# First batch of an attention and FFN kernel: block-transposed reciprocals, another order of its units, later weight loads, and more FFN work ahead of the third batch

## The chip, the cores and the metric

The kernel runs on one core of a Trainium2 chip. TensorE (PE in the profile, PEld for its weight loads), VectorE (DVE), ScalarE (ACT) and GpSimd (POOL) compute. SyncE (SP) and POOL issue DMAs. The metric is the time of one execution on the device in microseconds (us). The kernel before took 391.18 us, median of 6 runs (390.0 to 393.7). All other times come from one profiled execution.

## The reference

Attention over 8 batches and 8 heads of 576 queries, with 16 extra keys and values (the beacon) that every query sees; its output, as 4608 tokens by 512, goes through a gated FFN. Cut to what matters:

```python
k_all = concat([beacon_k, k]); v_all = concat([beacon_v, v])       # 592 keys
scores = (q @ k_all.T) / 8, causal on the 576 own keys
a = exp(scores - max); a /= a.sum(-1) + 1e-9
x = (a @ v_all) as [8*576, 8*64]
out = (relu(x @ w_gate) * (x @ w_val)) @ w_out                      # 512 -> 1536 -> 512
```

The result is float32. The kernel computes in bfloat16 with float32 sums.

## The kernel before

**Attention.** A batch has two groups g of four heads. Its 576 queries are cut into three chunks ci of 240, 256 and 80. A unit is one score tile: for a group and a chunk, the scores of one tile kt of 128 keys (small ones share a unit). Each batch has 14 units, two for each of its 7 steps. `Unit.qk` (L330) writes scores to one of two PSUM buffers s. `Unit.exp` (L341) takes exp on ACT (L344) into e, and POOL masks the diagonal (L352). When all units of a (g, ci) are through, `Chunk.av` (L364) multiplies: four heads side by side, 32 columns each, into the bank ab for the values and, with a tile of ones, into the bank os for the sums of exp. So each sum stands 32 times over, in the 32 partitions of its head. `Chunk.invert` (L390) takes the reciprocal of every element of os, and `Chunk.scale` (L395) multiplies ab by it into xT, the FFN's input. `Chunk.note` (L402) folds the reciprocals into a running minimum and maximum, which tell at the end whether a general path must run. ab and os have one buffer each. Chunks of the first batch's second group borrow two f banks or an s tile.

**FFN.** For each 512 tokens 12 up groups (`Ffn.up`, L412: four matmuls with wg at L419, four with wv at L428, relu on ACT, product on VectorE) and 4 down groups (`Ffn.down`, L432: 12 matmuls with wo at L438, a copy, a DMA to out). f banks: two.

**Order.** It is written by hand: `plan` (L474) is a list of steps, each with a batch and its part, or None where only FFN work runs, and a quota of FFN work. A whole-number quota counts groups; another one is in us of TensorE time. `ALONE` (L471) gives the steps without attention: four after the first batch (0, 3, 3 and 2 groups), two after the second (3 and 3). The third batch's steps have a quota of 3.0, later ones 4.4. `BASE` is the first step of each batch; s2, the second's, is step 11. Hooks hang on steps: `between` (behind the first unit's scores), `mid`, `behind`, and `after` (end of the step). Every engine runs its own instructions in this program order.

**Loads.** The first batch's q and k come in quarters (k or q, half i of the rows, group g), loaded by SP as float32 (wide), cast to bfloat16 (hwide), turned by TensorE (L282) and moved to kT and qT (L283). The last 64 rows, the tails, are turned in bank os (L305) and moved (L306). The second batch's quarters come through POOL's casting DMAs (L271), and are turned by TensorE in steps 10 (s2 - 1) and 12. The three weights come through POOL's queue too: `load_w` (L310) brings a third of wg or wv in two DMAs, `load_wo` (L316) half of wo. In POOL's order stand: first wg pair, first wv pair, second pairs, third pairs, the eight hwide loads, then a one-element memset (L227) on the buffer into which SP loads the second batch's first tile of v; SP's later DMAs stand behind that load. From the third batch on `fetch` (L631) loads float32 tiles of 128 rows on SP, POOL casts them (L249), and SP turns them by DMA transpose (L254), interleaved with the DMAs that write out. In these batches the second unit of a group needs key tile 3 and q tiles 2 and 3.

Of the kernel before, what the change touches and what calls it, by code (L numbers as in the profile page):

```python
# [10 lines left out]
FP32 = mybir.dt.float32  # L11
BF16 = mybir.dt.bfloat16
# [4 lines left out]
def general_path(tc, q, k, v, beacon_k, beacon_v, out, ident, wg, wv, wo):  # L17
# [119 lines left out]
)  # L137


UNITS_BY_CHUNK = (  # L140
    ((0, 0, 0),), ((0, 0, 1), (1, 0, 1)), ((1, 0, 0),), ((0, 1, 2),),
    ((0, 1, 3), (1, 1, 3)), ((0, 1, 1),), ((0, 1, 0),), ((1, 1, 2),), ((1, 1, 1),), ((1, 1, 0),),
# [11 lines left out]
def kernel(  # L154
# [12 lines left out]
    nc = tc.nc  # L167
    B, H, S, D = q.shape
    Nb = beacon_k.shape[2]
    P = 128  # L170
# [7 lines left out]
    M_TILE = 512  # L178
    C = 32
# [130 lines left out]
    def load_w(dst, src, n0, n1):  # L310
        for g in range(2):
            nc.gpsimd.dma_start(  # L312
                dst[:, 2 * g:2 * g + 2, n0:n1],
                src[2 * g * P:2 * (g + 1) * P, n0:n1].rearrange("(p a) n -> p a n", a=2))
# [42 lines left out]
    class Chunk:  # L357


        def __init__(self, batch, g, ci):  # L360
            self.batch, self.g, self.ci = batch, g, ci
            self.last = len(CHUNKS[ci][2]) - 1

        def av(self):  # L364
            spare = self.batch.b == 0 and self.g == 1
            if spare and self.ci == 2:
                s = s_ps.tile([P, 2, 2, 256], FP32, name="s")
                self.ab, self.os = s[:, 0], s[:, 1, 0]
            else:
                self.ab = (f_ps if spare else o_ps).tile(  # L370
                    [P, 2, 256], FP32, name="f" if spare else "ab")
                self.os = (f_ps if spare else o_ps).tile(
                    [P, 256], FP32, name="f" if spare else "os")
            cq0, _, segs = CHUNKS[self.ci]
            order = sorted(segs, key=lambda x: x[0])
            for i, (kt, q0, n, _, _) in enumerate(order):
                e = self.batch.e.pop((self.g, self.ci, kt))
                kr = min(P, Stot - kt * P)
                for part in range(3):
                    for hh in range(4):  # L380
                        rows = slice(hh * C, (hh + 1) * C)
                        c0 = (4 * self.g + hh) * D + part * C
                        w = ones[:kr, :] if part == 2 else self.batch.v[:kr, kt, c0:c0 + C]
                        o = self.os[rows] if part == 2 else self.ab[rows, part]
                        nc.tensor.matmul(  # L385
                            o[:, q0 - cq0:q0 - cq0 + n], w, e[:kr, 2 * (hh % 2) + hh // 2],
                            start=(i == 0 and part != 1), stop=(i == self.last),
                            skip_group_check=True)

        def invert(self):  # L390
            n = CHUNKS[self.ci][1]
            self.r = nrm.tile([P, 256], FP32, name="r")
            nc.vector.reciprocal(self.r[:, :n], self.os[:, :n])  # L393

        def scale(self):  # L395
            cq0, n, _ = CHUNKS[self.ci]
# [63 lines left out]
    def count_rows(ok):  # L460
# [7 lines left out]
    later_sp, pools = [], {}  # L468
    STEPS = 7

    ALONE = ((0, 3, 3, 2), (3, 3))  # L471
    BASE = [STEPS * b + sum(map(len, ALONE[:b])) for b in range(B)]

    plan = ([(0, i, 0) for i in range(STEPS)]  # L474
            + [(None, 0, n) for n in ALONE[0]]
            + [(1, i, 1) for i in range(STEPS)]
            + [(None, 0, n) for n in ALONE[1]]
            + [(b, i, 3.0 if b == 2 else 4.4) for b in range(2, B) for i in range(STEPS)]
            + [(None, 0, 4.5)])

    with tc.manual_schedule():
# [16 lines left out]
        def warm_up(count, n):  # L498
            for _ in range(count):
                nc.tensor.matmul(idle_ps[:, :n], wo[:, 0, :P], wo[:, 0, :n],  # L500
                                 start=True, stop=True)
# [12 lines left out]
        warm_up(4, M_TILE)  # L514
        first.turn_rows(first.cast_rows(first.beacon, dve), first.kT[:, :, :Nb], dve)()
        warm_up(2, M_TILE)
        def turn_first(i, g):
            for n in "kq":
                ps = f_ps.tile([P, 2, 2, P], BF16, name="f")
                first.turn_quarter(n, i, g, ps, act if n == "q" and g == 0 else dve)()  # L520
                if i == 0 and n == "k":
                    warm_up(1, 256)

        def cast_first(i, g):
            first.cast_quarter("k", i, g, dve)
            first.cast_quarter("q", i, g, dve if (i, g) == (1, 1) else act)

        cast_first(0, 0)
        turn_first(0, 0)
        warm_up(2, 256)  # L530
        cast_first(0, 1)

        def turn_two(x, i, k_bank):
            ps = {"k": k_bank.tile([P, NP, 2, P], BF16, name="f" if k_bank is f_ps else "s"),
# [9 lines left out]
        def turn_tails(x, move, ps=(None, None)):  # L544
            moves = [x.turn_rows(x.tails[0], x.kT[:, :, 528:592], move, ps[0]),
                     x.turn_rows(x.tails[1], x.qT[:, :, 512:576], move, ps[1])]
            for m in moves:
                m()

        def turn_first_tails():  # L550
            ps = o_ps.tile([P, 2, NP, 64], BF16, name="os")
            turn_tails(first, act, (ps[:, 0], ps[:, 1]))

        later_half, between, behind, mid = {}, {}, {}, {}

        def after(step, action):
            later_half.setdefault(step, []).append(action)
# [3 lines left out]
        load_tails(second)  # L561
        s2 = BASE[1]

        def turn_next():
            turn_first(0, 1)
            warm_up(2, 256)

        between[0] = turn_next
        mid[0] = lambda: cast_first(1, 0)
        after(0, lambda: cast_first(1, 1))  # L570
        after(0, lambda: first.cast("v", 0, pool))
        after(0, lambda: first.cast("v", 1, pool))
        def turn_last():
            turn_first(1, 0)
            ps = o_ps.tile([P, 2, 2, 2, P], BF16, name="ab")
            moves = []
            for x, n in enumerate("kq"):
                moves.append(first.turn_quarter(n, 1, 1, ps[:, x], dve))
                warm_up(1, (M_TILE, 256)[x])
            for move in moves:  # L580
                move()
            cast_tails(first, dve)

        between[1] = turn_last
        after(1, lambda: load_w(wg, moe_w_gate, 0, 512))
        after(2, lambda: first.cast("v", 2, pool))
        after(2, lambda: first.cast("v", 3, pool))
        after(2, lambda: load_w(wv, moe_w_val, 0, 512))
        behind[3] = turn_first_tails
        after(3, lambda: first.cast("v", 4, pool))  # L590
        after(3, lambda: load_w(wg, moe_w_gate, 512, 1024))
        after(4, lambda: load_w(wv, moe_w_val, 512, 1024))
        after(6, lambda: load_w(wg, moe_w_gate, 1024, 1536))
        after(6, lambda: load_w(wv, moe_w_val, 1024, 1536))

# [60 lines left out]
        for s, (b, i, quota) in enumerate(plan):  # L656
# [9 lines left out]
            if b is not None:  # L666
                if i == 0:
                    batches[b].e = {}
                order = UNITS_BY_CHUNK if b < 2 else UNITS_BY_GROUP
                units = [Unit(batches[b], order[2 * i + x]) for x in range(2)]  # L670
            chunks, due = due, []

            def values():
                for c in chunks:
                    c.av()
                    c.invert()
                    if b == 1:
                        c.scale()
                        notes.append(c.note)

            for j, u in enumerate(units):
                u.qk()
                if j == 0 and s in between:
                    between[s]()
                if j == 0 and s in (4, s2 + 1):
                    values()
            if units:
                units[0].exp()
            if units and s in mid:
                mid[s]()  # L690
            if s in behind:
                behind[s]()
            if s not in (4, s2 + 1):
                values()
            if s == STEPS:
                f = f_ps.tile([P, M_TILE], FP32, name="f")
                for _ in range(5):
                    nc.tensor.matmul(f, first.kT[:, 0, :P], first.kT[:, 0, :M_TILE],
                                     start=True, stop=True)
            credit = min(credit + quota, 2 * quota)  # L700
# [13 lines left out]
            for j, (kind, _, run) in enumerate(mine):  # L714
                if j == 0 and other and (kind == "down" or len(mine) == 1):
                    other.pop().exp()
                ups = kinds.count("up")
                run((b is None and j < len(mine) - 1) or (ups > 1 and j == (1 if ups > 2 else 0)))
                if j == 0:
                    for c in chunks if b != 1 else []:  # L720
                        c.scale()
                        notes.append(c.note)
                    if b is None and s in mid:
                        mid[s]()
                if other:
                    other.pop().exp()
                if b is None and notes:
                    notes.pop(0)()
            if not mine:
                for c in chunks if b != 1 else []:  # L730
                    c.scale()
                    notes.append(c.note)
                if other:
                    other.pop().exp()
# [59 lines left out]
```

## Time and profile before

| | |
|---|---|
| median of 6 runs | 391.18 us |
| the profiled execution's own time | 390.64 us |
| its span on the core | 388.9 us |
| busy PE / PEld / DVE / ACT / POOL | 369.4 / 187.7 / 204.8 / 192.0 / 124.2 us |
| PE busy in 16 to 26 us | 6.94 of 10 us |
| PE busy in 82 to 86 us | 1.60 of 4 us |
| moved by DMA | 49.85 MB, mean 128 GB/s |

The first 27 us are the first batch's attention, where no FFN input exists yet. From there FFN groups fill the time between the attention's pieces. TensorE's busy share is near 1 in most stretches, but the clock granted to it can be below full speed, so a busy stretch isn't always full work.

### The profile page before, as it was taken

To read this page: it belongs to the slowest core of one execution; us is meant where nothing else is said; L and a number is where in the kernel's file an instruction comes from. 1 tells how busy PE (TensorE), PEld (TensorE's weight loads), DVE (VectorE), ACT (ScalarE), POOL (GpSimd) and SP (SyncE) were. 2 spreads that over 40 slices of the span, in tenths; PEclk is the share of its full clock that TensorE was granted. 3 is DMA by queue.
4 is the path that set the end of the run, shared out by engine and by line. 5 is a ranking of instruction groups with operands and counts; after the bars stand their busy time and mean duration, and the time that the engine had idled before them with its cause. 6 is when DMAs were issued, how large, how long until landed. Compare 5 with 4: busy or idle time off the path is not lost.

```text
span 388.9 us, 10175 instructions
## 1 busy us (share of the span) xinstructions
PE 369.4 (95%) x4239; PEld 187.7 (48%) x4296; DVE 204.8 (53%) x333; ACT 192.0 (49%) x269; POOL 124.2 (32%) x217
## 2 busy tenths in 40 slices
PE   7779998979999999999999999999999999999995
PEld 3554454434554545445544545454544554444443
DVE  4878476535654566466446553666365654512320
ACT  4763493326655554565546545655465533323321
POOL 1795455325543442254225332335201100000000
PEclk9999999989999999999999999999999999999999
DMA  7999999759977872688267834786200020001002
GB/s 226 194 179 193 208 187 217 172 149 220 175 138 207 181 170 78 174 186 159 71 160 182 166 84 127 185 191 79 98 29 2 2 79 31 2 38 73 0 28 88
DMA packets 146788, 49.85 MB, mean 128 GB/s; under 512 B 133296, under 2 KB 142256, under 8 KB 146736
## 3 DMA queue, kind: packets, MB, share of 16 engines
q1 hardware_dynamic: 137680, 43.37, 47.6%
q0 software_dynamic: 9056, 5.77, 10.6%
q8 instruction: 35, 0.57, 0.7%
q14 instruction: 17, 0.14, 0.1%
HBM read 38.27 MB, written 9.44 MB: 123 GB/s over the span
## 4 chain that ended last, share of the span: by engine, by line
PE 81%; DMA 7%; POOL 4%; SPq 2%; issue 2%; DVE 1%; ACT 1%; POOLq 0%; DVEq 0%
PE f L438 24%; PE f L419 21%; PE f L428 10%; PE s L428 10%; PE s L336 6%; PE ab L385 6%; DMA wo<-in_moe_w_out_dram 3%; PE os L385 2%; DMA raw<-in_v_dram 2%; POOL e L352 1%; POOL v L245 1%; SPq L254 1%; DMA wide<-in_q_dram 1%; SPq L230 1%; POOL wg L312 1%
## 5 line engine op out<-in xcount | busy, mean ns | idle before, releaser
L344 ACT ACTIVATE e<-s 128x1024 bf16<-128x1024 f32 (+2 forms) x112 | 104.3, 966 | 23.3 <-PE s L336 23.3
L419 PE MATMUL f<-xT,wg 128*128 128x512 bf16 x407 | 110.0, 382 | 1.5 <-DVE hT L430 0.3
L422 ACT ACTIVATE g<-f 128x512 f32<-128x512 f32 x108 | 64.6, 598 | 88.2 <-PE f L419 82.6
L438 PE MATMUL f<-wo,hT 128*128 128x512 bf16 (+1 forms) x420 | 94.8, 373 | 3.6 <-issue 1.6
L352 POOL TENSOR_SCALAR_AFFINE_SELECT e<-e 128x512 bf16<-128x512 bf16 (+2 forms) x80 | 46.6, 595 | 153.7 <-ACT e L344 146.2
L393 DVE RECIPROCAL r<-os 128x240 f32<-128x240 f32 (+2 forms) x45 | 61.0, 1355 | 42.0 <-PE os L385 41.9
L430 DVE TENSOR_TENSOR hT<-g,f 128x512 bf16<-128x512 f32 x54 | 37.1, 688 | 60.1 <-PE f L428 54.3
L428 PEld LDWEIGHTS <-wv 128*128 128x128 bf16 x432 | 42.4, 98 | 52.7 <-issue 2.9
L430 DVE TENSOR_TENSOR hT<-g,s 128x512 bf16<-128x512 f32 x54 | 37.1, 688 | 58.3 <-PE s L428 55.2
L438 PEld LDWEIGHTS <-hT 128*128 128x128 bf16 x444 | 41.4, 98 | 47.9 <-issue 1.5
L419 PEld LDWEIGHTS <-wg 128*128 128x128 bf16 x432 | 40.1, 98 | 47.7 <-issue 1.9
L441 ACT COPY ob<-f 128x512 f32<-128x512 f32 (+1 forms) x37 | 21.3, 575 | 73.2 <-PE f L438 73.2
L428 PE MATMUL s<-xT,wv 128*128 128x512 bf16 x213 | 55.6, 382 | 0.1
L428 PE MATMUL f<-xT,wv 128*128 128x512 bf16 x213 | 55.1, 379 | 0.6 <-ACT qT L283 0.2
L249 POOL CAST half<-raw 128x512 bf16<-128x512 f32 (+2 forms) x60 | 36.1, 618 | 19.6 <-DMA raw<-in_q_dram 7.4
L385 PE MATMUL ab<-e,v 128*32 128x80 bf16 (+4 forms) x1320 | 38.7, 231 | 1.9 <-POOL e L352 1.0
L336 PE MATMUL s<-qT,kT 64*128 64x80 bf16 (+3 forms) x704 | 34.7, 231 | 4.8 <-DMA qT<-half 2.3
L336 PEld LDWEIGHTS <-kT 64*128 64x128 bf16 x704 | 20.4, 96 | 28.3 <-issue 25.7
L385 PE MATMUL os<-e,ones 128*32 128x240 bf16 (+4 forms) x660 | 31.7, 230 | 0.0
L385 PEld LDWEIGHTS <-v 128*32 128x32 bf16 (+1 forms) x1408 | 26.5, 97 | 10.6 <-issue 5.5
L245 POOL CAST v<-raw 128x512 bf16<-128x512 f32 (+1 forms) x40 | 26.2, 659 | 14.8 <-DMA raw<-in_v_dram 14.7
L398 DVE TENSOR_TENSOR xT<-ab,r 128x480 bf16<-128x480 f32 (+2 forms) x45 | 25.0, 555 | 1.0
(59 smaller groups left out, 130.3 us busy)
## 6 DMA issues: line engine op xcount, KB each, us to landing
out_dram<-ob SPq DMA_DIRECT2D x35, 256.0 KB, 2.3
raw<-in_v_dram SPq DMA_DIRECT2D x24, 256.0 KB, 4.8
raw<-in_q_dram SPq DMA_DIRECT2D x24, 256.0 KB, 4.3
raw<-in_k_dram SPq DMA_DIRECT2D x18, 256.0 KB, 3.8
raw<-in_v_dram SPq DMA_DIRECT2D x8, 224.0 KB, 3.7
wg<-in_moe_w_gate_dram POOLq DMA_DIRECT2D x6, 256.0 KB, 5.1
wv<-in_moe_w_val_dram POOLq DMA_DIRECT2D x6, 256.0 KB, 6.5
wo<-in_moe_w_out_dram POOLq DMA_DIRECT2D x2, 768.0 KB, 11.5
```

The source lines that it names most:

```text
L245: copy(self.v[:n, t].rearrange("p (h a d) -> p h a d", a=2, d=C), raw[:n].rearrange("p (h d a) -> p h a d", a=2, d=C))
L249: copy(h[:n], raw[:n])
L336: nc.tensor.matmul(self.s[:, a, c + j * n:c + (j + 1) * n], self.batch.kT[rows, 2 * g + j, kt * P:(kt + 1) * P], self.batch.qT[rows, 2 * g ...
L344: nc.scalar.activation(e[:, :k * 4 * n].rearrange("p (k a x) -> p a k x", k=k, a=2), self.s[:, :, :k * 2 * n].rearrange("p a (k x) -> p a ...
L352: nc.gpsimd.affine_select(out=cols[:, :, :m], in_=cols[:, :, :m], pattern=[[0, 4], [1, m]], compare_op=ALU.is_ge, fill=0.0, base=base, cha ...
L385: nc.tensor.matmul(o[:, q0 - cq0:q0 - cq0 + n], w, e[:kr, 2 * (hh % 2) + hh // 2], start=(i == 0 and part != 1), stop=(i == self.last), sk ...
L393: nc.vector.reciprocal(self.r[:, :n], self.os[:, :n])
L419: nc.tensor.matmul(g[:, :n], wg[:, ki, nf * P:(nf + 1) * P], x[:, ki], start=(ki == 0), stop=(ki == KM - 1))
L422: nc.scalar.activation(gs[:, :n], g[:, :n], AF.Relu)
L428: nc.tensor.matmul(u[:, :n], wv[:, ki, nf * P:(nf + 1) * P], x[:, ki], start=(ki == 0), stop=(ki == KM - 1))
L430: nc.vector.tensor_mul(self.h[:, nf, c0:c1], gs[:, :n], u[:, :n])
L438: nc.tensor.matmul(o[:, n], self.h[:, nf, ms * P:(ms + 1) * P], wo[:, nf, n], start=(nf == 0), stop=(nf == NF - 1))
```

## The change

- Chunks 0 and 1 of the first batch: `invert` transposes os in 32 by 32 blocks on VectorE, takes the reciprocal of one column in 32 (8 columns), and transposes it back, spread over 32. Chunk 0 has 240 queries; four small matmuls fill the other 16 columns.
- The first batch's units get an order of their own, `UNITS_FIRST`: (0, 1, 1) and (0, 1, 0) come ahead of the shared unit (0, 1, 3), (1, 1, 3). `HOLD` lets no chunk's values run in step 1 and one in step 2; in step 3 they come between the two units' scores, as in step 4.
- Turns of the first batch: the casts of k and q quarters and their moves are reordered. One q cast (half 1, group 0) and the moves of the tails go from ACT to VectorE; of the q moves, half 1 of group 0 goes to VectorE and half 0 of group 1 to ACT.
- The first wv load goes from the end of step 2 into step 3 (ahead of its second unit's mask), the second wg and wv loads from the ends of steps 3 and 4 to the end of step 6.
- In the first batch each chunk is scaled right after its reciprocal, as in the second.
- `ALONE[1]` is (4, 4) for (3, 3), and the third batch's quota is 2.6 for 3.0.
- Three filler matmuls (L698) for five ahead of the first FFN group.

```diff
+UNITS_FIRST = (
+    ((0, 0, 0),), ((0, 0, 1), (1, 0, 1)), ((1, 0, 0),), ((0, 1, 2),), ((0, 1, 1),), ((0, 1, 0),),
+    ((0, 1, 3), (1, 1, 3)), ((1, 1, 2),), ((1, 1, 1),), ((1, 1, 0),),
...
+            self.turned = batch.b == 0 and ci < 2
...
+                        if self.turned and i == 0 and part == 2 and n < 256:
+                            nc.tensor.matmul(o[:, n:], ones, ones[:, :256 - n],
+                                             start=False, stop=True, skip_group_check=True)
...
-            nc.vector.reciprocal(self.r[:, :n], self.os[:, :n])
+            if not self.turned:
+                nc.vector.reciprocal(self.r[:, :n], self.os[:, :n])
+                return
+            few = nrm.tile([P, 8], FP32, name="few", bufs=2)
+            nc.vector.transpose(self.r, self.os)
+            nc.vector.reciprocal(few, self.r[:, ::C])
+            nc.vector.transpose(self.r.rearrange("p (b c) -> p b c", c=C),
+                                few.unsqueeze(2).to_broadcast([P, 8, C]))
...
-    ALONE = ((0, 3, 3, 2), (3, 3))
+    ALONE = ((0, 3, 3, 2), (4, 4))
+    HOLD = {1: 0, 2: 1}
...
-            + [(b, i, 3.0 if b == 2 else 4.4) for b in range(2, B) for i in range(STEPS)]
+            + [(b, i, 2.6 if b == 2 else 4.4) for b in range(2, B) for i in range(STEPS)]
...
-            turn_tails(first, act, (ps[:, 0], ps[:, 1]))
+            turn_tails(first, dve, (ps[:, 0], ps[:, 1]))
...
         def turn_next():
-            turn_first(0, 1)
-            warm_up(2, 256)
+            turn_first("k", 0, 1, dve)()
+            first.cast_quarter("k", 1, 0, dve)
+            warm_up(1, 256)
+            held.append(turn_first("q", 0, 1, act))
+            first.cast_quarter("q", 1, 0, dve)
+        def turn_third():
+            held.pop()()
+            warm_up(1, 256)
+            turn_first("k", 1, 0, dve)()
+        between[0], mid[0] = turn_next, turn_third
+        behind[0] = lambda: turn_first("q", 1, 0, dve)()
...
-        between[1] = turn_last
+        behind[1] = turn_last
...
-        after(2, lambda: load_w(wv, moe_w_val, 0, 512))
         behind[3] = turn_first_tails
+        mid[3] = lambda: load_w(wv, moe_w_val, 0, 512)
         after(3, lambda: first.cast("v", 4, pool))
-        after(3, lambda: load_w(wg, moe_w_gate, 512, 1024))
-        after(4, lambda: load_w(wv, moe_w_val, 512, 1024))
+        after(6, lambda: load_w(wg, moe_w_gate, 512, 1024))
+        after(6, lambda: load_w(wv, moe_w_val, 512, 1024))
...
-                order = UNITS_BY_CHUNK if b < 2 else UNITS_BY_GROUP
+                order = (UNITS_FIRST, UNITS_BY_CHUNK)[b] if b < 2 else UNITS_BY_GROUP
...
-            chunks, due = due, []
+            n = HOLD.get(s, len(due))
+            chunks, due = due[:n], due[n:]
...
-                    if b == 1:
+                    if b in (0, 1):
...
-                if j == 0 and s in (4, s2 + 1):
+                if j == 0 and s in (3, 4, s2 + 1):
...
-                for _ in range(5):
+                for _ in range(3):
```

## The prediction

> **What bounds the kernel now.** I read the waits of TensorE first, because TensorE is busy for 95% of the span: from 27 us on, when the first FFN (feed-forward) group runs, it does one fixed amount of work and only its waits can be saved. Columns: total us, times, longest.
>
> ```profile
> PE s L336 <- DMA qT<-half: 2.3, 1, 2.3
> PE f L438 <- DMA wo<-in_moe_w_out_dram: 1.2, 1, 1.2
> ```
>
> Both wait for transfers. The chain of waits tells where those come from (start us, us, what):
>
> ```profile
> 22.26 1.38 POOL wg L312 x2
> 23.64 1.35 POOL wv L312 x2
> 24.99 0.08 issue
> 25.07 0.49 POOL e L352
> ...
> 37.50 0.74 POOL hwide L271
> 38.24 0.09 POOL raw L227
> 38.34 0.02 issue
> 38.35 0.32 SPq L230
> ...
> 49.21 12.01 DMA wo<-in_moe_w_out_dram
> ```
>
> POOL issues weights, then the second batch's casting loads (hwide); behind the last of these stands the one-element memset (L227) for which SP's loads of v wait. Single transfers, followed in the trace, land in a row without pause: the second wg pair at 26.7 and 28.0, the second wv pair at 29.9 and 31.1, the third pairs at 32.4, 33.7, 35.0 and 37.0, hwide one to four by 39.8, eight by 42.9. The last hwide is issued 0.5 us after the last wv has landed. Utilization by stretch says why (last columns: clock, DMA share, GB/s):
>
> ```profile
> 26.00:38.00 12.00, 11.89 (x102) 5.41 (x88) 9.28 (x23) 3.59 (x6) 8.51 (x12) 1.00 1.32 190
> 38.00:62.00 24.00, 21.35 (x275) 11.57 (x279) 15.72 (x24) 14.64 (x20) 10.64 (x20) 1.00 1.19 197
> ```
>
> The DMA engines are full from 22 to 62 us, and from 38.35 SP issues back to back up to 116 us, with no gap above 0.6 us. So one transfer chain runs from the weights to the fourth batch's transposes. The timeline shows where TensorE meets it:
>
> ```profile
> 85.71 0.40 PE L336 MATMUL s<-qT,kT 64*128 64x128 bf16 x4 [2.35 <-DMA qT<-half]
> 86.04 1.89 PE L419 MATMUL f<-xT,wg 128*128 128x512 bf16 x4
> ...
> 112.91 1.22 SPq L254 DMA_TRANSPOSE qT<-half  x1
> 115.69 0.60 PE L336 MATMUL s<-qT,kT 64*128 64x240 bf16 x12
> ```
>
> At the third batch's second unit TensorE waits 2.35 us for the transpose of q's fourth tile (landed 85.6); the granted clock falls to 0.5 and the next matmuls cost 0.86 + 0.51 + 0.1 = 1.45 us more (1.89 and 1.54 against 1.03). At the fourth batch the same tile lands 2.3 us after 112.91, at 115.2; it is used at about 115.95. Slack: 0.75 us.
>
> [...] 1747 ns for 256 columns, 648 for 80, 6.2 ns a column, against 1.03 for the multiplication (692 for 512, 326 for 160). [...]
>
> **The change, part by part.** *Reciprocals of the first batch's chunks 0 and 1:* 4 of 1.64 to 1.75 us go. Each becomes transpose, reciprocal of 8 columns (0.155 + 8 x 0.0062 = 0.2), transpose. A transpose of 256 columns is at least the memset of 128x256 f32, 0.27, and at most the reciprocal, 1.75; I take the row of the same size[...], 0.41 (least, 128x256)[...]. 1.05 instead of 1.7; with the scale of 0.66 a chunk's chain is 1.7 instead of 2.35. The 8 filler matmuls of 16 columns are 0.1 us where TensorE idles a third of the time (16 to 26 us: 6.94 of 10 busy); without that cover they cost the 0.1.
>
> *Tail moves from ACT to VectorE (2 x 0.28 there, 0.4 each on ACT):* they stand on VectorE behind both first chunk chains and hold the bank os that chunk (0,1) needs. VectorE is free from its casts at 15.6 to 16.0, as now (tail of q lands 15.1): 15.8 + 2 x 1.7 + 0.5 = 19.7. Now chunk (0,1) gets os at 19.2, behind ACT's moves. ACT reaches this point earlier (exps at 12.4 and 14.6 in place of 14.0 and 15.8, since a q cast and the tails are gone from it and a q move comes earlier), but unit 9's scores stand behind chunk (0,1) on TensorE: 19.7 + 1.0 of remaining matmuls + 0.4 = 21.1. Its exp starts then; scores of units 10 and 11, chunk (1,1) (1.3 us) and unit 12 follow: exp of 12 at 21.1 + 1.02 + 0.25 + 1.3 + 0.3 = 24.0, against 23.97 now. The exp of unit 13 ends at 25.5, the last values at 26.1, the 80-column reciprocal and scale (0.65 + 0.33) at 27.1. VectorE no longer carries a backlog here (its last scale ends 27.99 now), so the first FFN group is 0.9 us earlier. Two of five L698 matmuls go, inside this wait: nothing.
>
> *Weight loads:* the first pairs keep their place to 0.5 us. The second wg and wv pairs are moved from after steps 3 and 4 to after step 6: on POOL behind the masks of unit 12, whose exp ends at 24.9: 25.4 in place of 22.21. First landing after issue takes 4.1 to 4.5 us on an empty queue, so it lands at 29.7 instead of 26.7: 3.0 us late. The queue ran dry from 24.5 on, and what lands behind it is late by the same, less what closer spacing gives back (10.27 us for seven steps now, 8.9 at its usual 1.27): 1.6 to 3.0. I take 2.0. The second wv half then lands by 33.6, group 5 needs it at 34.6: hidden, just. The fourth hwide lands 41.8 and TensorE wants it at 41.5 - 0.9 = 40.6: the 0.9 gained is waited away. The memset, the v loads, both wo loads and SP's whole row of issues up to the fourth batch come 2.0 later: the wait for wo ends at 63.3, not 61.27.
>
> *Four groups in each of the two steps ahead of the third batch, quota 2.6 for 3.0 in it:* two up groups (2 x 1.73 = 3.46 us) come before the third batch. TensorE gets there 3.46 later than the chain, q's tile is 2.35 late now: the wait and the slow clock go, 2.35 + 1.45 = 3.8. By the instruction order 24 ups and 7 downs stand before the fourth batch now, 24 and 8 after: one down group (12 matmuls, 2.54) more is done by then. One out DMA (0.55 issue) moves ahead of the transposes of the fourth batch's fourth tile.
>
> **The sum.** After wo, TensorE reaches the fourth batch's second unit at 63.3 + (115.95 - 61.27) - 3.8 + 2.54 = 116.7; its tile lands at 115.2 + 2.0 + 0.55 = 117.75, so it waits 1.1 us[...]. What is left then is 388.9 - 115.95 - 2.54 = 270.4: end at 117.75 + 0.1 + 270.4 = 388.25, 0.65 under the profiled span. Each us of lateness of the stream is a us of the end: 386.25 + lateness. Outside the span the profiled run has 1.7 us; the median shown is 391.18, so 390.5.
>
> **Rivals.** *The stream catches up (faster):* landings every 1.27 us and masks of unit 12 done at 24.3 make the lateness about nothing; 386.2, 388.4 by the median. For it: six of eight spacings are 1.27. Against: exp 12 hangs on os. *No transfer binds at all:* 0.9 + 1.2 + 3.8 = 5.9 off, 385.3; against it are SP's 78 us without a gap. *VectorE's transposes are slow (slower):* they sit where os is held. At 1.3 us each a chain is 3.5 us, two chains put os, unit 12 and the weights 3.5 later: lateness 5.5, end 391.8, 394.0 by the median. Slower by over 0.5% starts at a lateness of 4.65, that is transposes of about 1.1.[...] *The change does nothing:* chunk chains shorter, os as late, lateness and the saved wait equal: that is my forecast's own neighbourhood.
>
> **Numbers.** Within 0.5% (about what a measurement here can tell from no change): 0.45, the forecast, lateness 0.4 to 4.6. Faster 0.37: the stream catches up 0.32, no binding 0.05. Slower 0.18. The likeliest case alone: 389.3 to 392.8. Low 386.8 leaves out half of the case without binding and a little more; high 394.0 is the slow transposes.
>
> **What would show it.** Right: chunk chains of 1.7 us on VectorE; os moved near 19.7; the second wg issued near 25.4; SP's first load of v after the memset near 40; no wait at the third batch and clock 1.0 there; about 1 us at the fourth; wo waited for again. Wrong: a wait above 2 us at the fourth batch with a dropped clock (+1.5), SP gaps before 116 us, or the weights landing as now.

## The result and the profile after

The changed kernel takes 393.8 us (median of 20 runs, 390.7 to 395.3) against 391.2 us for the kernel before, measured beside it. The ratio is 1.0059, 95% interval 1.0043 to 1.0076: slower by some 2.3 us. The forecast was 390.5, so the sign was wrong. The time lies inside the range, but only because its upper end (394.0) was drawn for a cause that turned out not to be there: luck. The profiled execution took 393.87 us with a span of 392.2, against 390.64 and 388.9. Line numbers of the changed kernel are 6 to 32 higher than before's.

The chain of waits, changed kernel (start us, us, what):

```profile
21.38 0.21 DVE qT L312
21.59 0.04 issue
21.64 0.29 PE os L392 x4
...
23.12 1.03 ACT e L350
...
26.14 0.16 ACT e L350
...
42.96 0.74 POOL hwide L277
43.70 0.09 POOL raw L233
...
43.81 0.32 SPq L236
```

In order: VectorE's move of the tails (L312) frees the bank os; chunk (0,1)'s sums (os L392) run; then the exp of unit 9 (23.12) and of unit 12 (26.14). The second wg pair follows on POOL at 27.68 instead of 22.21 before:

```profile
27.68 1.43 POOL L318 DMA_DIRECT2D wg<-in_moe_w_gate_dram  x2
```

At the end of the row POOL's memset (L233) stands at 43.70 instead of 38.24, and SP's first load of v at 43.81 instead of 38.35. The stream, that is the row of transfers from the weights to the fourth batch's transposes, is 5.46 us late. Landing times, followed in the trace as for before:

```text
            second wg      second wv      third wg       third wv
before    26.70  27.97   29.86  31.12   32.42  33.68   34.97  36.97
after     31.63  32.91   34.87  37.46   38.55  39.83   41.16  42.43
```

The utilization by stretch shows what happened to the DMA engines meanwhile (stretch, length, busy time of PE, PEld, DVE, ACT and POOL, then clock, DMA share, GB/s):

```profile
26.00:38.00 12.00, 11.09 (x177) 5.49 (x171) 9.41 (x23) 4.55 (x7) 8.67 (x13) 1.00 0.84 129
28.00:29.00 1.00, 0.95 (x57) 0.65 (x43) 0.97 (x3) 0.00 (x0) 1.00 (x2) 1.00 0.00 0
38.00:62.00 24.00, 20.78 (x241) 10.50 (x247) 13.55 (x24) 13.81 (x20) 12.99 (x22) 1.00 1.29 196
```

In 26 to 38 us the kernel before moved 190 GB/s, the changed one 129. Its queue had run dry: the first wv pair had landed by 26.43, POOL's next transfer landed at 31.63, and from 28 to 29 us nothing moved. From 38 to 62 us both are at the same rate (197 and 196), so nothing is caught up there. TensorE's waits show where the lateness arrives. In the timeline a line gives start, duration, engine, line, operation, tiles, shapes and count; in brackets stand the engine's idle time just before and what ended it.

```profile
PE os L392 <- DVE qT L312: 1.8, 1, 1.8
PE f L457 <- DMA wo<-in_moe_w_out_dram: 1.7, 1, 1.7
```

```profile
90.19 1.03 PE L447 MATMUL f<-xT,wv 128*128 128x512 bf16 x4
91.15 0.60 PE L342 MATMUL s<-qT,kT 64*128 64x240 bf16 x12
...
118.38 1.22 SPq L260 DMA_TRANSPOSE qT<-half  x1
...
120.81 0.29 PE L342 MATMUL s<-qT,kT 64*128 64x128 bf16 x4 [0.85 <-DMA qT<-half]
```

The 2.35 us wait at the third batch is gone (scores at 91.15 follow without one, clock 1.0). The fourth batch's transpose, issued at 112.91 before, is issued at 118.38: 5.47 us later, about the lateness at 43 us. TensorE waits 0.85 us for it and is from there on as late as it is. Most of the lateness had reached TensorE by then. Its wait for wo ends at 66.09 instead of 61.27, and the second batch's first exp starts 3.94 us later than before (changed kernel first):

```profile
48.37 1.88 ACT L350 ACTIVATE e<-s 128x960 bf16<-128x960 f32 x2 [0.93 <-PE s L342]
44.43 1.89 ACT L344 ACTIVATE e<-s 128x960 bf16<-128x960 f32 x2 [0.93 <-PE s L336]
```

### The profile page after: what moved, and what is told of

It is laid out like the page before. It is cut to its first block, busy times and chain, and to the rows that moved or that the text cites. A ratio compares the mean times of both kernels' runs of the same rounds, so it can differ in the third digit from the quotient of the medians.

```text
span 392.2 us, 10210 instructions
## 1 busy us (share of the span) xinstructions
PE 370.0 (94%) x4245; PEld 187.1 (48%) x4301; DVE 205.0 (52%) x344; ACT 191.1 (49%) x266; POOL 126.2 (32%) x217
## 4 chain that ended last, share of the span: by engine, by line
PE 76%; DMA 11%; SPq 4%; DVE 3%; POOL 3%; issue 2%; ACT 1%; POOLq 0%; DVEq 0%
PE f L457 21%; PE f L438 20%; PE s L447 12%; PE f L447 8%; PE s L342 5%; PE ab L392 5%; DMA raw<-in_q_dram 3%; DMA wo<-in_moe_w_out_dram 3%; PE os L392 2%; SPq L260 2%; SPq L236 2%; DMA raw<-in_v_dram 1%; DMA qT<-half 1%; DMA wide<-in_q_dram 1%; DMA raw<-in_k_dram 1%
## 5 line engine op out<-in xcount | busy, mean ns | idle before, releaser
L438 PE MATMUL f<-xT,wg 128*128 128x512 bf16 x405 | 108.9, 380 | 1.6 <-DVE hT L449 0.3
L404 DVE RECIPROCAL r<-os 128x80 f32<-128x80 f32 (+2 forms) x43 | 57.6, 1339 | 56.2 <-PE os L392 56.1
L449 DVE TENSOR_TENSOR hT<-g,s 128x512 bf16<-128x512 f32 x60 | 41.3, 688 | 66.0 <-PE s L447 64.9
L447 PE MATMUL s<-xT,wv 128*128 128x512 bf16 x238 | 61.6, 379 | 0.2
L449 DVE TENSOR_TENSOR hT<-g,f 128x512 bf16<-128x512 f32 x48 | 33.0, 688 | 36.1 <-PE f L447 28.9
L447 PE MATMUL f<-xT,wv 128*128 128x512 bf16 x186 | 48.8, 379 | 0.7 <-ACT qT L289 0.2
L255 POOL CAST half<-raw 128x512 bf16<-128x512 f32 (+2 forms) x60 | 37.5, 637 | 27.5 <-DMA raw<-in_q_dram 9.4
L392 PE MATMUL ab<-e,v 128*32 128x80 bf16 (+4 forms) x1320 | 38.8, 231 | 0.8 <-POOL e L358 0.7
L392 PE MATMUL os<-e,ones 128*32 128x240 bf16 (+4 forms) x660 | 31.8, 230 | 1.8 <-DVE qT L312 1.8
L392 PEld LDWEIGHTS <-v 128*32 128x32 bf16 (+1 forms) x1408 | 26.5, 97 | 10.6 <-issue 5.8
```

The source lines that it names most:

```text
L255: copy(h[:n], raw[:n])
L392: nc.tensor.matmul(o[:, q0 - cq0:q0 - cq0 + n], w, e[:kr, 2 * (hh % 2) + hh // 2], start=(i == 0 and part != 1), stop=(i == self.last), sk ...
L438: nc.tensor.matmul(g[:, :n], wg[:, ki, nf * P:(nf + 1) * P], x[:, ki], start=(ki == 0), stop=(ki == KM - 1))
L447: nc.tensor.matmul(u[:, :n], wv[:, ki, nf * P:(nf + 1) * P], x[:, ki], start=(ki == 0), stop=(ki == KM - 1))
L449: nc.vector.tensor_mul(self.h[:, nf, c0:c1], gs[:, :n], u[:, :n])
```

## The experiments

The stream theory: the end hangs on how late the weight stream is (the prediction's 386.25 plus lateness); moving the second pairs behind unit 12's mask is what made it late, and (4, 4) with 2.6 is a gain of its own. Rivals: the first batch's own slower start costs the time (first-batch theory); the (4, 4) part costs it (four-groups theory); the reciprocals do (reciprocal theory). Each ratio below is to the kernel before, measured beside it; 0.1% is 0.39 us. "Lateness" is that of the last wv landing in the profiled execution against before's 36.97. Single executions of one kernel lie up to 3.7 us from its median, and their streams differ too. Two kernels below have the same program up to the end of the second batch (reciprocals alone, and with four groups); their profiled executions landed the last wv at 37.75 and 35.71. So a lateness, read from one execution, is good to about 2 us. Verdicts rest on the ratios; the traces show the mechanism.

### The second pairs, put back

```diff
-        after(6, lambda: load_w(wg, moe_w_gate, 512, 1024))
-        after(6, lambda: load_w(wv, moe_w_val, 512, 1024))
+        after(3, lambda: load_w(wg, moe_w_gate, 512, 1024))
+        after(4, lambda: load_w(wv, moe_w_val, 512, 1024))
```

> Stream theory (the end is 386.25 plus the lateness of the weight stream): second pairs issued near 23.1 instead of 27.7, so the last wv lands near 37.9 instead of 42.4, lateness 0.9, and the span is 387.2 to 387.7, about 0.4% faster than the kernel before. First-batch theory (the cost is VectorE's late chunk chains and the FFN work that starts 1.6 us later): both stay as they are, so the span stays at 391.5 to 392.5. Four-groups theory (the redistribution before the third batch costs the time): the same, 391.5 to 392.5.

Ratio 0.9956 (0.9937 to 0.9975), 389.6 us. Issued at 22.42, lateness 1.38. The first FFN group still starts late (29.6), and the kernel is yet faster than before: two lines of order are worth 1.0% of the kernel, 4.0 us, for 4.1 us of lateness. The profiled execution (span 390.2) was slower than expected, and 2.3 us slower than its kernel's median; the ratio came as expected. Both rivals miss.

### The second pairs, moved alone

The reverse edit, made in the kernel before.

> Stream theory: in the kernel before, unit 12's mask ends near 25.3, so the second wg pair is issued at about 25.4, 3.2 us later than now, and the last wv lands 3.2 to 3.8 us later. TensorE waits that much longer at the third batch, so the span is 391.7 to 392.8, 0.7 to 1.0% slower. First-batch theory and four-groups theory: neither of their causes is in this kernel, 388.5 to 389.5.

Ratio 1.0086 (1.0065 to 1.0107), 3.4 us. Lateness 2.46, less than expected. TensorE meets part of it at the third batch:

```profile
88.59 0.29 PE L336 MATMUL s<-qT,kT 64*128 64x128 bf16 x4 [3.51 <-DMA qT<-half]
88.81 1.15 PE L419 MATMUL f<-xT,wg 128*128 128x512 bf16 x4
89.75 1.91 PE L428 MATMUL s<-xT,wv 128*128 128x512 bf16 x4
```

The wait grows from 2.35 to 3.51 us, and the slow clock after it stays (1.91 where 1.03 is usual). TensorE is late before that, too: the third batch's first exp starts at 85.01, before at 83.29. First-batch and four-groups theories expected no change.

### Four groups, alone

```diff
-    ALONE = ((0, 3, 3, 2), (3, 3))
+    ALONE = ((0, 3, 3, 2), (4, 4))
...
-            + [(b, i, 3.0 if b == 2 else 4.4) for b in range(2, B) for i in range(STEPS)]
+            + [(b, i, 2.6 if b == 2 else 4.4) for b in range(2, B) for i in range(STEPS)]
```

> Stream theory: lateness 0, so 386.25 and nothing added: span 386.0 to 386.9, 0.5 to 0.7% faster; no wait of 2 us at the third batch, clock 1.0 there. Four-groups theory: this part is what costs, 390.5 to 392. A third possibility, what is saved at the third batch is given back at the fourth: 388.4 to 389.4, with a wait of over 2 us there.

Ratio 0.9931 (0.9907 to 0.9954), 388.8 us: the fastest of all. No wait at the third batch, clock 1.0; the fourth batch's tile lands at 114.21, just as TensorE comes for it. The prediction's formula asked for 2.65 us less than before (388.9 to 386.25); the ratio says 2.7. The profiled execution (span 384.9, below the expected range) was the quickest of its six.

### Four groups, taken out of the changed kernel

The reverse edit, made in the changed kernel.

> The changed kernel with (3, 3) and 3.0 as before. Stream theory: the late stream now meets TensorE at the third batch again, where it waits over 2 us and its clock drops, so the kernel before plus the lateness of 4.8 to 5.5: ratio 1.012 to 1.014. Four-groups theory (this part is what costs): below the changed kernel, ratio 1.000 to 1.003. If this part does nothing: 1.006, as the changed kernel.

Ratio 1.0112 (1.0083 to 1.0142), a little below what the stream theory expected. Its wait at the third batch is 2.10 us, and this time the clock stays up:

```profile
90.70 0.29 PE L342 MATMUL s<-qT,kT 64*128 64x128 bf16 x4 [2.10 <-DMA qT<-half]
90.92 1.04 PE L438 MATMUL f<-xT,wg 128*128 128x512 bf16 x4
91.80 1.03 PE L447 MATMUL s<-xT,wv 128*128 128x512 bf16 x4
```

So this part is worth 0.5% in the changed kernel and 0.7% alone. The intervals don't tell these apart; the slow clock (some 1.5 us in the kernel before), which was expected here and didn't come, would account for the difference. Lateness 5.65.

### The second pairs one step earlier

```diff
-        after(6, lambda: load_w(wg, moe_w_gate, 512, 1024))
-        after(6, lambda: load_w(wv, moe_w_val, 512, 1024))
+        after(5, lambda: load_w(wg, moe_w_gate, 512, 1024))
+        after(5, lambda: load_w(wv, moe_w_val, 512, 1024))
```

> The changed kernel with its second pairs one step earlier. Stream theory: issued near 25.6, 2.1 us earlier than in the changed kernel, lateness 3.3, span 389.5 to 390.2, within 0.3% of the kernel before; so each us of lateness is a us of the end. Unit 12's mask now stands behind the four transfers' issue, so the FFN starts up to 1.2 us later. First-batch theory: 392.5 to 393.5, because the FFN starts later still.

Ratio 0.9994 (0.9973 to 1.0015), issued at 24.78, lateness 2.58. With the changed kernel and the pairs put back it makes a row:

```text
lateness, us                  1.38    2.58    5.46
386.25 + lateness - 388.9    -1.27   -0.07   +2.81
measured (ratio x 391.3)     -1.72   -0.23   +2.31
```

The steps between neighbours agree to 0.4 us, within the intervals of some 0.8 us. That is closer than three single executions can promise: this one took 393.13 us, 1.5 more than its kernel's median.

### The tails moved by ACT

```diff
-            turn_tails(first, dve, (ps[:, 0], ps[:, 1]))
+            turn_tails(first, act, (ps[:, 0], ps[:, 1]))
```

> The changed kernel with the tails moved by ACT as before. If the bank os, held for the tail moves behind two chunk chains on VectorE, is what delays unit 12 and with it the weights: os is free near 19 to 19.7, 1.9 earlier, the exp of unit 12 and the second wg pair come 1.5 to 2 earlier, the lateness is 2.8 to 3.6, ratio 0.999 to 1.002. If os isn't what delays them: the second wg pair within 0.4 us of the changed kernel's and ratio 1.005 to 1.007.

Ratio 1.0019 (1.0002 to 1.0035): 0.4% or 1.6 us under the changed kernel. The timeline of ACT shows the tails between two exps, and that of POOL what follows:

```profile
17.54 0.37 ACT L312 COPY kT<-os 128x256 bf16<-128x256 bf16 x1
17.81 0.38 ACT L312 COPY qT<-os 128x256 bf16<-128x256 bf16 x1
18.07 4.34 ACT L350 ACTIVATE e<-s 128x1024 bf16<-128x1024 f32 x5
22.95 1.56 ACT L350 ACTIVATE e<-s 128x960 bf16<-128x960 f32 x2 [0.54 <-PE s L342]
...
24.49 1.42 POOL L318 DMA_DIRECT2D wg<-in_moe_w_gate_dram  x2
```

TensorE's 1.8 us wait on os is gone, ACT no longer pauses ahead of unit 9, and unit 12's exp starts at 22.95 instead of 26.14. The second wg pair is issued 3.2 us earlier and the lateness is 1.95, both better than expected. But this was the quickest execution of its kernel (389.36 us, median 392.33) and its first loads came 0.67 us earlier, so not all of the 3.2 us belongs to the edit.

### The same with the pairs put back

> The changed kernel with the second pairs put back behind steps 3 and 4 and the tails moved by ACT. The weights come as in the run with the pairs put back alone (lateness 0.9 to 1.4), and the bank os comes free 1.9 us earlier, so the FFN starts near 27.0 to 27.7 instead of 29. Stream theory: a us of the end for each of lateness, ratio 0.995 to 0.997, whatever the FFN's start. If, with the stream nearly on time, TensorE's own start is what counts: 1.9 us less than in the run with the pairs put back alone, ratio 0.989 to 0.992.

Ratio 0.9962 (0.9947 to 0.9978), the same as with the pairs put back alone (0.9956), though the FFN starts at 27.75 instead of 29.6. Lateness 0.57. An earlier start of the FFN buys nothing that intervals of 0.2% would show. The place of the tails matters through the weights that stand behind unit 12.

### Transposed reciprocals, alone and with four groups

```diff
+            self.turned = batch.b == 0 and ci < 2
...
-            nc.vector.reciprocal(self.r[:, :n], self.os[:, :n])
+            if not self.turned:
+                nc.vector.reciprocal(self.r[:, :n], self.os[:, :n])
+                return
+            few = nrm.tile([P, 8], FP32, name="few", bufs=2)
+            nc.vector.transpose(self.r, self.os)
+            nc.vector.reciprocal(few, self.r[:, ::C])
+            nc.vector.transpose(self.r.rearrange("p (b c) -> p b c", c=C),
+                                few.unsqueeze(2).to_broadcast([P, 8, C]))
```

Made in the kernel before:

> The kernel before with the transposed reciprocals alone. Stream theory: VectorE does 2.4 us less in the first batch and the FFN starts 0.3 to 1.2 us earlier, but the weights are issued as before and the third batch's tile lands as before: ratio 0.998 to 1.001. Reciprocal theory (VectorE's time there reaches the end): 0.994 to 0.996.

Made in the kernel with four groups alone:

> The kernel before with (4, 4), 2.6 and the transposed reciprocals. Stream theory: TensorE reaches the fourth batch's fourth tile of q just as it lands when (4, 4) and 2.6 stand alone, so an earlier FFN start is waited away there: ratio 0.991 to 0.995, as without the transposes. Reciprocal theory: 0.986 to 0.990.

Ratios 1.0009 (0.9989 to 1.0029) and 0.9942 (0.9922 to 0.9962), against 1 and 0.9931 without them: no difference that can be measured, twice. The reciprocals' time on VectorE does not reach the end.

### An earlier first wg pair

```diff
-        after(1, lambda: load_w(wg, moe_w_gate, 0, 512))
+        after(0, lambda: load_w(wg, moe_w_gate, 0, 512))
```

Made in the kernel with four groups and transposed reciprocals, behind the first two casts of v:

> The kernel before with (4, 4), 2.6 and the transposed reciprocals, and with the first wg pair two masks earlier, behind the first two v casts. POOL's idle stretch of 0.7 us goes, and the stream comes 0.5 to 0.9 us earlier. Stream theory: 0.5 to 0.9 us less than in the same kernel without it, ratio 0.991 to 0.993. If TensorE alone sets the end there: 0.993 to 0.996, as without it.

Ratio 0.9943 (0.9921 to 0.9964), as without it (0.9942). The stream did not come earlier, so this doesn't tell the two theories apart. It even came later: the last wv landed at 38.35, without the edit at 35.71 (and at 37.75 in the same program with three groups). Taken at their word, 2.6 us of lateness cost nothing here. But the execution without the edit was the quickest of its kernel (386.25 us, median 388.87), so its 35.71 isn't typical. POOL's timeline says why the stream gained nothing:

```profile
23.13 0.65 POOL L245 CAST v<-raw 80x512 bf16<-80x512 f32 x1 [1.49 <-DMA raw<-in_v_dram]
23.72 1.43 POOL L312 DMA_DIRECT2D wg<-in_moe_w_gate_dram  x2
```

SP's last tile of v, issued at 14.68 between the two wg transfers, landed at 23.08, after both of them (21.07 and 22.89). Its cast, ahead of the second pairs on POOL, waited 1.49 us, and these were issued at 23.72 instead of 20.91 (22.93 with three groups).

### The memset ahead of the last four hwide loads

```diff
-        after(7, lambda: load_second(1))
         for t in range(NKT):
             after(7, lambda t=t: second.load("v", t, t == 0))
+        after(7, lambda: load_second(1))
```

> The changed kernel with the one-element memset, and so SP's loads of v, ahead of the last four hwide loads instead of behind them. The weights stay as late as they are. If the lateness reaches the end through SP's row of issues: SP's first load of v near 38.6 instead of 43.8, the fourth batch's fourth tile of q lands 3 to 5 us earlier, ratio 0.993 to 0.999. If it reaches the end through TensorE's own waits for weights and hwide loads between 28 and 62 us: as the changed kernel, ratio 1.004 to 1.008.

Ratio 1.0068 (1.0034 to 1.0102): no gain, as in the second of the two cases. SP did start 4.75 us earlier, at 39.06, but look at its five v loads. Changed kernel, then this one:

```profile
44.17 6.02 SPq L236 DMA_DIRECT2D raw<-in_v_dram  x5
50.24 0.51 SPq L236 DMA_DIRECT2D raw<-in_beacon_k_dram  x1
```

```profile
39.42 10.86 SPq L236 DMA_DIRECT2D raw<-in_v_dram  x5
50.33 1.85 SPq L236 DMA_DIRECT2D raw<-in_beacon_k_dram  x1
```

They take 10.86 us instead of 6.02, and SP is at its next load at 50.3 in both. The fourth batch's tile lands at 121.19, against 120.76. TensorE now waits 4.2 us for hwide loads instead of some 1.6 (total us, times, longest), and then not noticeably for that tile:

```profile
PE s L288 <- DMA hwide<-in_k_dram: 2.3, 2, 1.3
PE f L288 <- DMA hwide<-in_q_dram: 1.9, 2, 1.0
```

So neither SP's place in the order nor the memset carries the lateness. One supply for POOL's transfers and SP's loads would fit all of this: SP's five v loads took 4.84 us longer, TensorE's waits for hwide grew by 2.6 us, and the changed kernel and this one moved the same 167 GB/s over 16 to 62 us. That is an estimate from these numbers: no run here shows the supply by itself or separates it from TensorE's own waits for hwide. Over 16 to 62 us the utilization is, for before, changed and this kernel in turn:

```profile
16.00:62.00 46.00, 40.18 (x629) 22.52 (x636) 34.13 (x55) 27.23 (x38) 29.12 (x47) 1.00 1.21 190
```

```profile
16.00:62.00 46.00, 38.79 (x628) 21.12 (x631) 30.30 (x63) 25.52 (x35) 29.23 (x46) 1.00 1.09 167
```

```profile
16.00:62.00 46.00, 36.93 (x588) 20.28 (x588) 28.40 (x60) 22.48 (x31) 28.47 (x45) 0.96 1.13 167
```

23 GB/s less over 46 us is 1.06 MB not moved. At 190 GB/s that is 5.6 us: the lateness once more, counted in bytes, and no second proof of it. The same figure is 191 with four groups alone, 189 with the pairs put back, 184 one step earlier, 181 with the pairs moved alone and 166 with three groups put back: the order of the latenesses (-0.09, 1.38, 2.58, 2.46, 5.65), but for two neighbours. For the small ones the bytes say less than the landings (189 is 0.2 us, not 1.38).

## Why the prediction was wrong

**The step that failed: "I take 2.0" for the lateness.** It measured 5.46. Two terms of it were mis-sized: the first landing came 4.93 us late, not 3.0, and closer spacing gave back nothing, where taking 2.0 counted on 1.0; the spacing cost another 0.53 (4.93 + 0.53 = 5.46).

*The issue of the second pairs, 25.4 forecast, 27.68 measured.* "VectorE is free from its casts at 15.6 to 16.0, as now" was wrong: the first chunk chain starts at 17.57, 1.77 us after the forecast's 15.8. That is most of the 2.28. VectorE's timeline:

```profile
12.16 0.69 DVE L289 COPY qT<-f 128x512 bf16<-128x512 bf16 x1 [0.42 <-PE f L288]
12.76 1.60 DVE L273 CAST hwide<-wide 128x512 bf16<-128x512 f32 x2
...
16.43 1.21 DVE L303 CAST half<-raw 64x512 bf16<-64x512 f32 x2
17.57 0.43 DVE L409 STREAM_TRANSPOSE r<-os 128x256 f32<-128x256 f32 x1
18.04 0.20 DVE L410 RECIPROCAL few<-r 128x8 f32<-128x8 f32 x1
18.28 0.45 DVE L411 STREAM_TRANSPOSE r<-few 128x256 f32<-128x256 f32 x1
```

The first q quarter landed at 5.78 instead of 5.14, ahead of anything that the change moves; the executions with three groups put back and with the memset moved show the same (5.78, 5.79), the one with the pairs put back doesn't (5.16). What decides it stays open. But two casts took 1.60 us where two took 0.75 before, and the other order puts them there: they stand beside a pair of masks on POOL (12.68 to 14.09), in before they had no POOL work beside them. I moved work between engines and took its price from a place where the neighbour was idle. In the execution with the pairs put back, whose first three quarters came on time, the casts are again 1.60 and the chain starts at 17.02. There VectorE even waited for the chunk's sums:

```profile
17.02 0.45 DVE L409 STREAM_TRANSPOSE r<-os 128x256 f32<-128x256 f32 x1 [0.67 <-PE os L392]
```

TensorE ends these sums at 16.97 there and at 17.35 in the changed kernel, before at 15.44. In its order the turns of the last quarters, which need those casts, stand ahead of them. So a VectorE that was free at 15.8 would have found no sums to work on, which the forecast left out. From the chain on the working held: two chains, 1.76 us from start to start (forecast 1.7), tail moves to 21.58, the os matmul at once, unit 12's exp 4.5 us later (forecast 4.3). With the tails on ACT this late VectorE no longer reaches the weights through them, which gave back 1.6 us.

*"What closer spacing gives back", up to 1.4 us, 1.0 of it counted on.* Nothing came: from the first landing of the second pairs to the last of the third took 10.8 us, before 10.27. The lower end of 1.6 rested on this.

**The formula held, roughly.** 386.25 + 5.46 = 391.7, the span was 392.2. All kernels with (4, 4), by the lateness of their profiled executions:

```text
                                         lateness, us    ratio
four groups and reciprocals                 -1.26       0.9942
four groups alone                           -0.09       0.9931
pairs put back, tails on ACT                 0.57       0.9962
pairs put back                               1.38       0.9956
four groups, reciprocals, first wg early     1.38       0.9943
tails on ACT                                 1.95       1.0019
pairs one step earlier                       2.58       0.9994
changed kernel                               5.46       1.0059
memset ahead of four hwide loads             5.91       1.0068
```

A straight line through these nine rises by about 0.8 us of time for each us of lateness, and single points lie up to 1.3 us off it. So that lateness of the weights costs time is shown, by the pairs moved to and fro; that it costs one us for each is an estimate. How it gets to the end was told wrong in part: not through SP's place behind the memset. What the runs show fits DMA time that is lost while the queue is dry (0 GB/s from 28 to 29 us) and isn't made up afterwards: from 38 to 62 us the changed kernel moved 196 GB/s at a DMA share of 1.29, before 197 at 1.19. TensorE meets it in its waits for hwide and wo before it meets it in the fourth batch's tile.

**Point by point.** Transposes 0.43 to 0.45 us, forecast 0.41: right, and the rival that priced them at 1.3 falls. That it named the lateness and the time that came about (5.5, 394.0) is luck. The 0.41, VectorE's time for least at 128x256, was an estimate: no row of the kernel before shows a transpose on VectorE. The reciprocal of 8 columns took 0.20, as worked out from before's reciprocals (1747 ns for 256 columns, 648 for 80). Third batch's wait and slow clock gone: right, also when made alone (0.86 + 0.51 + 0.1 makes 1.47, not 1.45; it changes nothing). ACT's exps forecast at 12.4 and 14.6 started at 13.6 and 16.09, the second of them late behind these casts and turns. Wait at the fourth batch 1.1: 0.85, at a clock of 1.00 (118 to 124 us). FFN 0.9 us earlier: it is 1.6 later (27.46 to 29.07), for the same reason as the weights, and of no measurable account by the run with early pairs and tails on ACT. Wait for wo ends at 63.3: wo lands at 66.05. The chance of a catch-up (0.32) was too high: before's stretches already showed DMA shares of 1.32 and 1.19 up to 62 us, and the changed kernel moved no more than before from 38 to 62 us (196 and 197 GB/s).

The parts, from the runs: four groups -2.7 us (alone), reciprocals nothing, late pairs +3.4 (alone) to +4.0 (in the changed kernel), of which 1.6 through the tails on VectorE. Together that is +1.3, against +2.3 measured. What is left, the new order of units, casts and moves and the later first wv load, was not tried alone. It is about 0.2% between the tails-on-ACT kernel with early pairs (0.9962) and the one with four groups and reciprocals (0.9942), which is within the intervals and stays open. Better than both kernels is the one before with (4, 4) and 2.6 alone: 0.9931.

## What to carry to other kernels

Look for a queue of transfers that runs dry ahead of a busy stretch: here nothing moved from 28 to 29 us, the DMA share was 1.29 from 38 to 62, and about 0.8 us of the end went with each us of lateness, some 350 us ahead of it. Starting SP's loads 4.75 us earlier gained nothing (ratio 1.0068 against 1.0059). When a load is hung behind a mask or an exp, follow what that instruction itself waits for, bank by bank, before pricing the move. Price an instruction that changes place by its row beside the neighbours it will have there (two casts: 0.75 us in one place, 1.60 in the other). And before reading a rule off single executions, see how far two executions of one program lie apart.

## What the runs showed of the hardware

- Two float32 to bfloat16 casts of 128x512 on VectorE took 0.75 us with nothing on POOL (kernel before, at 9.85) and 1.60 beside two affine selects on POOL (changed kernel at 12.76, pairs put back at 11.93), which themselves took 1.41 in both, where two took 1.23 in the kernel before. No run here separates POOL's work from other causes.
- A wait of TensorE of 2.10 us (three groups put back) left the granted clock at 1.00 (mean of 84 to 100 us; matmuls 1.04 and 1.03). At the same place 2.35 us (kernel before) and 3.51 us (pairs moved alone) were followed by slow matmuls (1.89 and 1.91), and with reciprocals alone 2.8 us went with the same mean clock, 0.89 from 84 to 100 us in all three. In the kernel before the granted clock was 0.50 from 86 to 88 us. Between 2.10 and 2.35, 0.25 us more of waiting went with another 1.5 us of slow matmuls; each is one execution. The 1.23 us that TensorE waited for wo in the kernel before (until 61.27) left the clock at 1.00 (59 to 63 us). No run here shows where between these waits the clock drops, or whether the length of the wait alone decides it.
- Each of POOL's last six hwide loads is issued 0.3 to 0.5 us after the landing of its transfer eight places earlier (the last one at 42.96 after 42.43, before 37.50 after 36.97). So a late stream also delays the issue of what follows. No run here shows whether the program or the queue asks for this wait.
